# Precedence for VectorE's additions on read-outs of the projection, blocks 2 to 5, in a fused attention and SwiGLU kernel

## The chip, the cores and the metric

The kernel runs on one core of a Trainium2 chip. The metric is the device time of one execution in microseconds (us), as the median of several runs. The core's engines have a queue each: TensorE (PE; its weight loads are listed apart as PEld), VectorE (DVE), ScalarE (ACT), GpSimd (POOL) and SyncE (SP). Each queue is worked off in its own order, and semaphores hold an instruction until what it needs is done.

## The reference

```python
# q, k, v: (8, 8, 576, 64)  batch, heads, positions, head size; float32
scores = scale * q @ k.T                      # per batch and head
scores += -slope[h] * abs(i - j)              # ALiBi
attn = softmax(where(0 <= i - j < 128, scores, -1e9))
x = (attn @ v)  -> (4608, 512)                # tokens x (heads * head size)
g, val = x @ w_gate, x @ w_val                # 512 -> 1536
out = (g * sigmoid(g) * val) @ w_out          # 1536 -> 512
```

So it is a sliding-window attention of 128 positions, followed by a gated feed-forward block. The last product, 1536 to 512, is called the projection here.

## The kernel before

**Blocks.** The 4608 tokens are worked on as nine blocks of 512. The code counts them from 0 (`n`), this text from 1: blocks 2 to 5 are `n` = 1 to 4. For each block the attention makes `x`, which is transposed into `xT`. Then the gate (`pg`) and value (`pv`) products follow (L397, 128x512 tiles). ScalarE applies tanh (L415, `tt`). VectorE makes `uu = (tt + 1) * pg` (L416) and `hT = uu * pv` (L427).

**Projection with seven products.** From the second block on, the projection is done by a seven-product scheme in place of eight (the function `strassen`), in two passes `t` of 128 token columns each. It needs sums of parts of `hT`, which VectorE makes (L485 to L488, tiles `S2`, `S3`, `S4`, and in place in `hT`), and its seven products of six matmuls each (L532) read these sums. Pass by pass the products run so:

| product | into | read out by |
|---|---|---|
| first | `X` | ScalarE, to `p1s` |
| second | `p2`, a bank of its own | VectorE: `half_plus`, with `p1s` |
| third, on `S2` | `X`, added | ScalarE, to `u2s` |
| fourth | `Y` | ScalarE, to `p5s` |
| fifth, on `S3` | `X`, added | VectorE: `half_plus`, with `p5s` |
| sixth, on `S4` | `Y`, added | VectorE: `half_plus`, with `u2s` |
| seventh | `X`, added | ScalarE |

`X` and `Y` are the two halves of one PSUM bank:

```python
po = ps_f.tile([P, 2, HC], FP32, name="po", tag="po", bufs=1)
X, Y = po[:, 0, :], po[:, 1, :]
```

`p2` of blocks 2 to 5 comes from the pool `ps_a`, which has four banks. The same four banks hold the attention's scores (`ps` L278, `psc` L313) and its weighted values (`av` L345). VectorE frees an `av` bank with a reciprocal and a multiplication (L347, L348, tile `x`). VectorE also multiplies the exponentials with the mask (L290 `ex`, L321 `exc`). The products of block `n` - 1 are mixed into the gate and value products of block `n`, and attention for later blocks runs in between. Sums of weights (L597 to L600) are made on VectorE too, from the sixth block on in the program's text, into `kT`, `qT` and mask tiles that are no longer needed; they are read by products of blocks 7 to 9 (L623).

**Who sets the order.** A first part of the program, up to step 60 of the feed-forward steps, has a hand-written order on PE, VectorE and ScalarE. From there on, only PE's order is written by hand; the order on VectorE and ScalarE is chosen when the program is built, by a scheduler that takes, of the instructions that it holds to be ready, the one with the highest priority:

```python
fixed.enter_context(tc.manual_schedule(engines=ENGINES["pe"]))
```

Normally priority follows the order in which the program is written. `tc.high_priority()` lifts what is written under it above the rest. `half_plus` is L535 and L536.

Of the kernel before, what the change touches and what calls it, by code (L numbers as in the profile page):

```python
# [13 lines left out]
ALU = mybir.AluOpType  # L14
# [17 lines left out]
SEVEN_FROM = 6  # L32
# [19 lines left out]
def kernel(  # L52
# [10 lines left out]
    nc = tc.nc  # L63
# [377 lines left out]
    def store(n, j, osb, c0=0, c1=512, two=False):  # L441
        for i, (p0, p1, r0) in enumerate(rows_of(n, j)):
            (nc.scalar if two and i else nc.sync).dma_start(out[r0:r0 + p1 - p0, c0:c1],
                                                            osb[p0:p1, c0:c1])
# [59 lines left out]
    def strassen(n, t):  # L504

        h = hT[n]
        A11, A12 = h[:, 0:HM, 0:256], h[:, HM:NMB, 0:256]
        S1, A22 = h[:, 0:HM, 256:512], h[:, HM:NMB, 256:512]
        S2, S3, S4 = hsum[n]
        cols = slice(t * P, (t + 1) * P)  # L510
        end = n == NBLK - 1
        seeded = SEVEN_FROM <= n + 1 < NBLK
        factor = 1.0 if n >= SEVEN_FROM else 0.5
        if end:
            X, Y = (ps_a.tile([P, HC], FP32, name="po", tag="a", bufs=4) for _ in range(2))
            p2 = ps_f.tile([P, HC], FP32, name="p2", tag="gv")
        else:
            po = ps_f.tile([P, 2, HC], FP32, name="po", tag="po", bufs=1)
            X, Y = po[:, 0, :], po[:, 1, :]
            p2 = (ps_f.tile([P, HC], FP32, name="p2", tag="gv") if seeded  # L520
                  else ps_a.tile([P, HC], FP32, name="p2", tag="a"))
        top, low = (opool.tile([P, DM], FP32, name="osb", tag="osb") for _ in range(2))
        if end and t:
            spare = [opool.tile([P, DM], FP32, name="osb", tag="osb") for _ in range(2)]
            p1s, p5s, u2s = spare[0][:, 0:HC], spare[0][:, HC:DM], spare[1][:, 0:HC]
        else:
            p1s, p5s, u2s = (supool.tile([P, HC], FP32, name=i, tag=i, bufs=1)
                             for i in ("p1s", "p5s", "u2s"))

        def product(dst, a, b, start=False):  # L530
            for m in range(HM):
                nc.tensor.matmul(dst, a[:, m, cols], b[:, m, :], start=(start and m == 0),  # L532
                                 stop=(m == HM - 1), skip_group_check=True)

        def half_plus(dst, a, b):  # L535
            nc.vector.scalar_tensor_tensor(out=dst, in0=a, scalar=factor, in1=b,  # L536
                                           op0=ALU.mult, op1=ALU.add)

        product(X, A11, B11, True)
        if seeded:  # L540
            nc.scalar.copy(p2, X)
        else:
            nc.scalar.mul(p1s, X, factor)
        yield
        product(p2, A12, B21, not seeded)
        if seeded:
            nc.vector.tensor_scalar_mul(top[:, 0:HC], p2, factor)
        else:
            half_plus(top[:, 0:HC], p2, p1s)
        if end and t:  # L550
            store(n, t, top, 0, HC)
        yield
        product(X, S2, T2)
        nc.scalar.mul(u2s, X, factor)
        yield
        product(Y, S1, T1, end)
        if end and t:
            nc.vector.tensor_scalar_mul(p5s, Y, factor)
        else:
            nc.scalar.mul(p5s, Y, factor)  # L560
        yield
        product(X, S3, T3)
        half_plus(low[:, HC:DM], X, p5s)
        if end and t:
            store(n, t + 2, low, HC, DM, True)
        yield
        product(Y, S4, B22)
        half_plus(top[:, HC:DM], Y, u2s)
        store(n, t, top, HC if end and t else 0, DM, end)
        yield  # L570
        product(X, A22, T4)
        if end:
            nc.vector.tensor_scalar_mul(low[:, 0:HC], X, factor)
        else:
            nc.scalar.mul(low[:, 0:HC], X, factor)
        store(n, t + 2, low, 0, HC if end and t else DM, end)
        yield
# [427 lines left out]
```

## Time and profile before

| | before |
|---|---|
| median of 6 runs | 345.23 us (344.74 to 345.55) |
| profiled execution, time | 345.42 us |
| profiled execution, span in the trace | 343.6 us |
| PE busy | 329.9 us (96%) |
| VectorE busy | 277.4 us (81%) |
| ScalarE busy | 207.6 us (60%) |
| granted TensorE clock | 1.0 |

Times in the trace are counted from the start of the span. "Busy" is the time in which an engine works on something. A group of instructions is named by line, engine, operation and its tiles, out<-in. In a timeline, each row has the start, the time from the first start to the last end, the engine, line, operation, tiles and count, and in brackets the idle time of the engine before it with the instruction that ended it. The modelled ends of matmuls overlap the start of the next ones a little.

### The profile page before, as it was taken

What the parts mean: (1) busy time and instruction counts of PE and PEld (TensorE: products, weight loads), DVE (VectorE), ACT (ScalarE), POOL (GpSimd) and SP (SyncE); (2) the same over time, 40 slices, a digit from 0 to 9 for tenths busy, and PEclk for the clock granted to TensorE, in tenths of its full rate; (3) what the DMA queues carried; (4) which work ended last, traced back from release to release, by engine and by line L of the source; (5) the groups of instructions that cost most, each with busy time, mean ns of one, the idle gap of its engine ahead of it and who ended that gap; (6) DMA issues with size and microseconds to landing.
All of it is one profiled execution on the core that took longest, in us unless ns stands there. A gap on an engine that the chain in (4) does not pass through costs nothing.

```text
span 343.6 us, 7778 instructions
## 1 busy us (share of the span) xinstructions
PE 329.9 (96%) x2983; PEld 218.6 (64%) x2983; DVE 277.4 (81%) x652; ACT 207.6 (60%) x412; POOL 109.6 (32%) x136
## 2 busy tenths in 40 slices
PE   7999999999999999999999999999999999999995
PEld 3584445444456565556565655565788878888884
DVE  5477985999798669998899999999855875775683
ACT  3748676465766665656555547563467666776640
POOL 8977672648774274744017000000000000000000
PEclk9999999999999999999999999999999999999999
DMA  9999999999999999999999912021101101011014
GB/s 149 168 180 177 162 169 151 78 139 153 132 173 137 159 169 165 144 165 134 160 199 99 183 30 82 15 63 47 63 2 61 62 1 64 2 62 63 0 68 118
DMA packets 160037, 37.37 MB, mean 109 GB/s; under 512 B 147328, under 2 KB 155648, under 8 KB 160000
## 3 DMA queue, kind: packets, MB, share of 16 engines
q0 software_dynamic: 118336, 18.62, 85.5%
q1 hardware_dynamic: 40976, 17.64, 28.3%
q10 hardware_dynamic: 688, 0.62, 0.6%
q8 instruction: 23, 0.38, 0.5%
q14 instruction: 14, 0.11, 0.1%
HBM read 37.91 MB, written 9.44 MB: 138 GB/s over the span
## 4 chain that ended last, share of the span: by engine, by line
PE 68%; DVE 20%; ACT 6%; issue 3%; DMA 2%; SPq 0%; DVEq 0%; ACTq 0%
PE po L532 14%; PE pg L397 12%; PE pv L397 12%; PE gX L623 8%; PE gY L623 4%; PE av L345 4%; DVE uu L416 3%; DVE hT L427 3%; PE ps L278 3%; PE p L532 2%; DVE x L348 2%; PE gZ L623 2%; DVE ex L290 2%; ACT ex L284 2%; PE po L451 2%
## 5 line engine op out<-in xcount | busy, mean ns | idle before, releaser
L397 PE MATMUL pv<-xT,wv_sb 128*128 128x512 f16 (+2 forms) x320 | 76.5, 358 | 0.6 <-DVE uu L416 0.3
L397 PE MATMUL pg<-xT,wg_sb 128*128 128x512 f16 (+2 forms) x320 | 75.8, 358 | 0.3 <-DVE xT L373 0.2
L415 ACT ACTIVATE tt<-pg 128x512 f16<-128x512 f32 (+2 forms) x70 | 41.3, 590 | 50.5 <-PE pg L397 49.5
L284 ACT ACTIVATE ex<-ps 128x512 f16<-128x512 f32 x96 | 50.0, 606 | 12.0 <-PE ps L278 12.0
L416 DVE SCALAR_TENSOR_TENSOR uu<-tt,pg 128x512 f16<-128x512 f16 (+2 forms) x69 | 46.1, 668 | 10.4 <-ACT tt L415 10.2
L427 DVE TENSOR_TENSOR hT<-uu,pv 128x512 f16<-128x512 f16 (+2 forms) x70 | 46.8, 668 | 3.6 <-PE pv L397 1.6
L185 POOL DMA_DIRECT2D va<-in_v_dram x40 | 34.3, 861 | 34.4 <-PE av L345 26.9
L397 PEld LDWEIGHTS <-wg_sb 128*128 128x128 f16 x320 | 28.2, 98 | 24.4 <-issue 2.2
L397 PEld LDWEIGHTS <-wv_sb 128*128 128x128 f16 x320 | 28.3, 98 | 24.1 <-issue 3.0
L532 PEld LDWEIGHTS <-hT 128*128 128x128 f16 x384 | 36.8, 98 | 10.4 <-issue 1.1
L191 POOL DMA_DIRECT2D kn<-in_k_dram x39 | 33.2, 854 | 20.9 <-DMA kT<-kn 11.1
L191 POOL DMA_DIRECT2D qn<-in_q_dram x39 | 33.3, 860 | 19.7 <-DMA va<-in_v_dram 11.7
L532 PEld LDWEIGHTS <-S 128*128 128x128 f16 x288 | 27.7, 98 | 10.6 <-issue 2.5
L290 DVE TENSOR_TENSOR ex<-ex,m_reg 128x1024 f16<-128x1024 f16 x42 | 28.7, 689 | 3.2 <-ACT ex L284 3.1
L348 DVE TENSOR_TENSOR x<-av,rec 128x256 f16<-128x256 f32 x72 | 28.6, 420 | 0.4
L532 PE MATMUL po<-T,S 128*128 128x256 f16 x192 | 26.5, 273 | 0.5 <-DVE S L487 0.5
L532 PE MATMUL po<-T,hT 128*128 128x256 f16 x192 | 26.1, 273 | 0.0
L317 ACT ACTIVATE exc<-psc 128x512 f16<-128x512 f32 x40 | 21.3, 608 | 4.1 <-PE psc L313 4.1
L675 DVE TENSOR_TENSOR hT<-s,v 128x512 f16<-128x512 f16 x18 | 7.6, 425 | 18.5 <-ACT s L674 18.5
L345 PEld LDWEIGHTS <-ex 128*128 128x128 f16 x384 | 17.4, 97 | 4.6 <-issue 1.3
L345 PE MATMUL av<-va,ex 128*128 128x65 f16 x384 | 19.3, 193 | 0.7 <-ACT ex L284 0.7
L278 PE MATMUL ps<-qT,kT 64*128 64x256 f16 x192 | 16.6, 272 | 0.4 <-DVE qT L223 0.2
(134 smaller groups left out, 536.9 us busy)
## 6 DMA issues: line engine op xcount, KB each, us to landing
out_dram<-osb SPq DMA_DIRECT2D x32, 256.0 KB, 2.6
va<-in_v_dram POOLq DMA_DIRECT2D x32, 128.0 KB, 8.8
qn<-in_q_dram POOLq DMA_DIRECT2D x31, 128.0 KB, 8.8
kn<-in_k_dram POOLq DMA_DIRECT2D x31, 128.0 KB, 9.1
wg_sb<-in_moe_w_gate_dram POOLq DMA_DIRECT2D x6, 256.0 KB, 7.8
wv_sb<-in_moe_w_val_dram POOLq DMA_DIRECT2D x6, 256.0 KB, 8.3
wo_sb<-in_moe_w_out_dram POOLq DMA_DIRECT2D x2, 768.0 KB, 9.7
kn<-in_k_dram POOLq DMA_DIRECT2D x8, 64.0 KB, 7.2
```

Source lines behind the costliest of these rows:

```text
L185: nc.gpsimd.dma_start(va[rank][p0:p1, :, 0:D], src)
L191: nc.gpsimd.dma_start(t_[p0:p1], src)
L284: nc.scalar.activation(e[:, o:o + 2, :], banks[q4][par], AF.Exp, scale=scale)
L290: nc.vector.tensor_mul(e[:, o, :], e[:, o, :], reg[:, o, :])
L345: nc.tensor.matmul(av[:, j, :], w, val, start=(n == 0), stop=(n == len(todo) - 1))
L348: nc.vector.tensor_mul(x[:, 4 * half:4 * half + 4, :], av[:, :, 0:D], rec.broadcast_to([P, 4, D]))
L397: nc.tensor.matmul(ps[:, c0:c1], w[:, kb, ms], xT[n][:, kb, c0:c1], start=(kb == 0 and c0 == 0), stop=(kb == NKB - 1 and c1 == 512), skip_ ...
L415: nc.scalar.activation(tt, pg[:, c0:c1], AF.Tanh, scale=0.5)
L416: nc.vector.scalar_tensor_tensor(out=uu, in0=tt, scalar=one if (n, m) == PIN else 1.0, in1=pg[:, c0:c1], op0=ALU.add, op1=ALU.mult)
L427: nc.vector.tensor_mul(hT[n][:, m, c0:c1], acted[(n, m)][1][:, c0:c1], pv[:, c0:c1])
L532: nc.tensor.matmul(dst, a[:, m, cols], b[:, m, :], start=(start and m == 0), stop=(m == HM - 1), skip_group_check=True)
L623: nc.tensor.matmul(dst[:, i, :], w[:, kb, c0 + i * P:c0 + (i + 1) * P], a[:, kb, :], start=(start and i == 0 and kb == 0), stop=(i == 1 an ...
```

## The change

```diff
         def half_plus(dst, a, b):
-            nc.vector.scalar_tensor_tensor(out=dst, in0=a, scalar=factor, in1=b,
-                                           op0=ALU.mult, op1=ALU.add)
+            with tc.high_priority() if n + 1 < SEVEN_FROM else ExitStack():
+                nc.vector.scalar_tensor_tensor(out=dst, in0=a, scalar=factor, in1=b,
+                                               op0=ALU.mult, op1=ALU.add)
```

`SEVEN_FROM` is 6, so the 24 additions of `n` = 1 to 4 are lifted: four blocks, two passes, three additions each. The instructions of the program stay the same. In the built program the queues of PE, ScalarE, GpSimd and SyncE stand in the same order as before. On VectorE, the same 652 working instructions are there, and 93 of them stand at another place of the queue, between about 110 and 240 us of the trace before.

## The prediction

> **What bounds the kernel now.** I read the page first, then who waits for the changed line, then the stages, then both engines' timelines at each place where TensorE (PE) waits for VectorE.
>
> ```profile
> PE 329.9 (96%) x2983; PEld 218.6 (64%) x2983; DVE 277.4 (81%) x652; ACT 207.6 (60%) x412; POOL 109.6 (32%) x136
> PE 68%; DVE 20%; ACT 6%; issue 3%; DMA 2%; SPq 0%; DVEq 0%; ACTq 0%
> ```
>
> PE is busy for 96% of the span and carries 68% of the chain that ended last. VectorE carries 20% of it: there PE stood and waited for VectorE. PE's queue does not change, so the change can gain or lose only at such waits. The view of line 536 (the additions) ends with those who waited for it:
>
> ```profile
> who waited for it (us, times):
>   PE po L532: 1.5, 2
>   PE psc L313: 0.2, 1
> ```
>
> So three visible waits, 1.7 us together: about the most that this change can bring. The stages show how full VectorE is there (columns: window, length, then busy time and count of PE, PEld, DVE, ACT, POOL):
>
> ```profile
> 98.00:190.00 92.00, 89.81 (x841) 54.89 (x840) 81.72 (x190) 57.09 (x116) 42.05 (x51) 1.00 1.94 155
> 190.00:246.00 56.00, 55.33 (x480) 33.27 (x478) 54.39 (x135) 28.90 (x57) 0.00 (x0) 1.00 0.35 67
> ```
>
> PE idles for 2.2 us and 0.7 us in them; VectorE is busy for 54.39 of 56 us in the second. So an addition that goes first pushes back something that PE may need next. The waits, on PE:
>
> ```profile
> 167.55 0.39 PE L371 MATMUL px<-idm,x 128*128 128x128 f16 x4
> 168.56 0.82 PE L532 MATMUL po<-wo_sb,S 128*128 128x256 f16 x6 [0.62 <-DVE osb L536]
> ...
> 182.21 0.61 PE L278 MATMUL ps<-qT,kT 64*128 64x256 f16 x8
> ...
> 189.35 0.81 PE L532 MATMUL po<-wo_sb,S 128*128 128x256 f16 x6 [0.84 <-DVE osb L536]
> ...
> 218.65 0.39 PE L532 MATMUL po<-T,S 128*128 128x256 f16 x2 [0.52 <-DVE S L487]
> 218.98 0.45 PE L313 MATMUL psc<-qT,kT 64*128 64x128 f16 x9
> 219.58 0.38 PE L313 MATMUL psc<-qT,kT 64*128 64x128 f16 x7 [0.15 <-DVE osb L536]
> ```
>
> and VectorE's queue ahead of them:
>
> ```profile
> 141.73 0.42 DVE L487 TENSOR_TENSOR S<-hT 128x512 f16<-128x512 f16 x1
> 142.07 0.69 DVE L321 TENSOR_TENSOR exc<-exc,m_reg 128x1024 f16<-128x1024 f16 x1
> 142.67 0.42 DVE L536 SCALAR_TENSOR_TENSOR osb<-p,p1s 128x256 f32<-128x256 f32 x1
> ...
> 167.49 0.68 DVE L427 TENSOR_TENSOR hT<-uu,pv 128x512 f16<-128x512 f16 x1
> 168.08 0.42 DVE L536 SCALAR_TENSOR_TENSOR osb<-po,p5s 128x256 f32<-128x256 f32 x1
> ...
> 188.28 0.68 DVE L416 SCALAR_TENSOR_TENSOR uu<-tt,pg 128x512 f16<-128x512 f16 x1
> 188.88 0.42 DVE L536 SCALAR_TENSOR_TENSOR osb<-po,p5s 128x256 f32<-128x256 f32 x1
> ```
>
> The additions of the last two rows read `X` (with `p5s`). They stand behind an `uu` or `hT` step, while PE's next product waits to write `Y` in the same bank.
>
> **Slots.** Consecutive VectorE instructions start 0.085 us before the one ahead ends: 142.67 to 143.00 is a slot of 0.34 for an addition of 0.42, 168.08 less 167.49 is 0.59 for an `hT` of 0.68. PE's held instruction starts about 0.05 after VectorE's end (168.08 + 0.42 = 168.50, start 168.56). With these rows I follow the new order of VectorE's queue against the old and keep one number: PE's offset against before.
>
> **The change part by part.** It adds and removes no instruction; each of the 24 additions keeps its 0.42 us. Six places matter.
>
> A, 110.95 us: an addition passes a reciprocal (slot 0.09), and PE's wait of 0.03 ends. Offset -0.03.
>
> B, 141.73: the addition on `p2` is now put ahead of the sum `S2` (L487) and `exc`. `S2` comes 0.34 later, less the 0.02 of A. PE's weight loads of `S` are just in time now (six take 0.75 us at 141.65, and 0.53 at 168.56), so PE stands: offset +0.32. The next load that waits for an `x` step (at 144.03, idle 0.21 before it in PEld's timeline) finds it done as early as before, since all three moved steps stand ahead of it in both orders; that wait of 0.20 vanishes. Offset +0.12.
>
> C, 168.56: the addition passes `hT` (0.59), and VectorE is 0.12 late from B, because its last idle ahead (0.56 at 165.40) ends by ScalarE's `exc`, which follows PE. So it starts 0.47 earlier. PE's wait, start to start, is 168.56 less 167.55 less 0.28 (four such transposes at 110.64, next at 110.95, less A's 0.03) = 0.73. Of it 0.73 - 0.12 - 0.47 = 0.14 stays. Offset -0.47, a step of -0.59.
>
> D, 182.21: PE would come 0.47 early to the scores tile whose bank `x` frees at 181.80 + 0.42 = 182.22. VectorE shows no idle worth naming between 166 and 194, and this `x` has the same steps ahead of it in both orders (an `ex` half moves 2 us back, but still stands before it), so `x` cannot come earlier. The fifth weight load stands at about 182.34, only 0.06 after the release. So 0.41 is given back: offset -0.06.
>
> E, 189.35: the addition passes `uu` (0.60), and a weight sum (L597, 0.34) that stood ahead at 185.26 goes behind it. It starts near 187.96 and ends at 188.38, before PE needs it: the first load of `S` is at 188.44, its matmul 0.11 later (the spacing of these matmuls), so the product starts at 188.55 less D's 0.06 = 188.49 instead of 189.35. Offset -0.87, a step of -0.81.
>
> Is E kept? Behind it VectorE idles in the old order by 0.13, 0.45, 0.11, 0.31, 0.05 and 0.11 us at 194.62, 195.76, 196.90, 200.30, 201.71 and 205.21 (each start less the end before it), 1.16 in sum, and three of these end by ScalarE's `tt` or `exc`, which follow PE. That is room for 0.87.
>
> F, 218.65: the addition on `p2` passes eight steps, among them one `x` and `S2`. `S2` comes 0.87 - 0.33 = 0.54 earlier only, and PE waits longer for it: offset -0.54. In return the wait of `psc` for this addition ends. Matmuls of L313 follow each other by some 0.027 (sixteen in 0.62 at 105.70); the tenth stands at 219.58 instead of 218.98 + 9 x 0.027 = 219.22, so 0.36 is won. Offset -0.90.
>
> Behind 220 us no PE wait hangs on a moved step: the moved weight sums and sums of `xT` are read from 246 us on, and the masked `ex` half of D is written by 181.9 and read by PE's weighted values at 184.28 at the earliest. Stores of the output by SyncE follow the additions and wait for no one on the path. Sum: **-0.9 us**. The profiled execution took 345.42 (span 343.6 and 1.8 around it), and 0.19 over the median; I take the step from the median: 345.23 - 0.9 = **344.3**.
>
> Bounds: the smallest C + D is 0 (all given back), and E lies between 0 and 0.90 (the 0.84 of idle and the 0.06 of overlap). B + F lie between -0.4 (the S2 delays hidden) and +0.65 (no return of either). I take the worked values, since each rests on rows at its own place.
>
> [...] The row says that VectorE is busy for 54.39 of 56 us from 190 on and idles 1.16 us in 189 to 205. [...] I go by the idle row. In B and F the delay is a slot of 0.34 by the rows. [...]
>
> **The rivals.** (1) *Given back.* VectorE is full from 166 to 194 and nearly so to 240, and E's gain returns as PE's wait for `S2` at 218.65. For it: that wait exists, 0.52 us. Against it: the idle of 1.16. The time: -0.9 + 0.81 = -0.1, so 345.1. (2) *S2 pushed back, slower.* Additions go ahead of the sums that the next product reads, at B (+0.35, 0.20 of it returned) and F (+0.33, unreturned if `psc` is really held by something else). It decides if the waits of C and E were held by a second release close behind the addition, say ScalarE's copy of the same bank. Then the sum is -0.03 + 0.15 + 0.33 = +0.45: 345.7, and 345.9 if B's 0.20 does not return either. Against it: both rows name the addition, and PE starts 0.05 after its end. (3) *It does nothing.* The scheduler's order could already be best; but the queues differ at the named places. 345.2.
>
> **How the numbers follow.** The forecast has 0.76, rival 1 has 0.16, rival 2 has 0.05, rival 3 has 0.03. What a measurement of this kernel can tell from no change is about 0.2%, 0.69 us. The forecast's own range is 343.9 to 344.7; the six runs spread over 0.8, so a median may bring a fifteenth of its chance, 0.05, to within 0.2%. So faster 0.76 - 0.05 = 0.71; within 0.2% 0.05 + 0.16 + 0.03 = 0.24; slower 0.05. The range runs from 343.8 (the S2 delays hidden) up to the middle of rival 1, 345.1: it leaves out half of that rival, the other two and the forecast's edges, under 0.2 together.
>
> **What would show it.** Right: PE's idle before the products near 168 and 188.5 falls to at most 0.2 us and to none; `S2` waits of PE near 142 and 218 grow by 0.3; a new wait of L278's load for `x` near 182; the additions' row of waiters falls from 1.7 to about 0.2; PE's last instruction 0.9 us earlier. Wrong: E's place still held, by a ScalarE copy or a sum, or PE's offset against before returns to near 0 at 218.

## The result, and the profile after

| | before | after |
|---|---|---|
| median | 345.32 us (48 runs) | 344.17 us (23 runs) |
| ratio, 95% interval | | 0.9969 (0.9959 to 0.9978) |
| span of the profiled execution | 343.6 us | 342.7 us |

The change saves 1.07 us by the ratio (0.76 to 1.42); the two medians differ by 1.15. The forecast was 0.9.

In the page after, PE is as busy as before in microseconds, in a shorter span, and the chain that ended last holds less of VectorE (17% for 20%):

```profile
PE 329.7 (96%) x2983; PEld 218.6 (64%) x2983; DVE 276.8 (81%) x652; ACT 207.6 (61%) x412; POOL 109.6 (32%) x136
PE 66%; DVE 17%; DMA 10%; issue 3%; ACT 2%; POOL 1%; ACTq 0%; DVEq 0%; POOLq 0%
```

The view of the additions' line, now 537, names no one any more who waited for it; before it named PE with 1.5 and 0.2 us. The stages (same columns as before) show PE busy 1.25 us longer from 98 to 190, with VectorE as before:

```profile
who waited for it (us, times):
busy tenths in 40 slices 0000000000000000000000000000000000000011
```

```profile
98.00:190.00 92.00, 91.06 (x846) 55.23 (x845) 81.67 (x190) 57.42 (x117) 41.37 (x50) 1.00 1.77 155
190.00:246.00 56.00, 55.15 (x484) 33.76 (x483) 54.82 (x137) 29.09 (x59) 0.00 (x0) 1.00 0.27 67
```

Now the six places, first VectorE's queue. At B the addition stands ahead of `S2`, at C ahead of `hT`, at E ahead of `uu`, with the weight sum (now L598) behind it:

```profile
141.53 0.42 DVE L537 SCALAR_TENSOR_TENSOR osb<-p,p1s 128x256 f32<-128x256 f32 x1
141.87 0.42 DVE L487 TENSOR_TENSOR S<-hT 128x512 f16<-128x512 f16 x1
...
167.44 0.41 DVE L537 SCALAR_TENSOR_TENSOR osb<-po,p5s 128x256 f32<-128x256 f32 x1
167.77 0.68 DVE L427 TENSOR_TENSOR hT<-uu,pv 128x512 f16<-128x512 f16 x1
...
187.79 0.42 DVE L537 SCALAR_TENSOR_TENSOR osb<-po,p5s 128x256 f32<-128x256 f32 x1
188.13 0.68 DVE L416 SCALAR_TENSOR_TENSOR uu<-tt,pg 128x512 f16<-128x512 f16 x1
188.72 0.42 DVE L598 TENSOR_TENSOR qT<-wv_sb,wg_sb 128x512 f16<-128x512 f16 x1
```

PE's weight loads, where the two new waits are (B and D):

```profile
142.34 0.11 PEld L532 LDWEIGHTS <-S 128*128 128x128 f16 x2 [0.36 <-DVE S L487]
...
181.59 0.22 PEld L278 LDWEIGHTS <-kT 64*128 64x128 f16 x5 [0.42 <-issue]
182.12 0.11 PEld L278 LDWEIGHTS <-kT 64*128 64x128 f16 x3 [0.31 <-DVE x L348]
```

and PE at C, E and F:

```profile
167.49 0.39 PE L371 MATMUL px<-idm,x 128*128 128x128 f16 x4
167.91 0.82 PE L532 MATMUL po<-wo_sb,S 128*128 128x256 f16 x6
...
188.27 0.81 PE L532 MATMUL po<-wo_sb,S 128*128 128x256 f16 x6
...
217.90 0.39 PE L532 MATMUL po<-T,S 128*128 128x256 f16 x2 [0.85 <-DVE S L487]
218.22 0.62 PE L313 MATMUL psc<-qT,kT 64*128 64x128 f16 x16
```

The idle of 0.62 and 0.84 us at C and E is gone. PE's wait for `S2` at F has grown from 0.52 to 0.85, and the sixteen `psc` matmuls run through.

**One caution in reading.** Single profiled executions differ in their first 60 us, where no instruction has moved: the `pv` product at 109.78 before starts at 109.65 after, 0.13 earlier, and in the experiments' traces 0.2 to 0.7 earlier. So I compare the starts of the same matmul (PE's queue is the same in all kernels) and take off the offset that it has at that `pv`. Second traces of two of the kernels (the full change and the additions after the fifth product, both run again below) repeat their rows of the table within 0.03 us. The offset behind each place, in us:

| behind place | A | B | C | D | E | F | last matmul |
|---|---|---|---|---|---|---|---|
| forecast | -0.03 | +0.12 | -0.47 | -0.06 | -0.87 | -0.90 | -0.90 |
| after | -0.07 | +0.07 | -0.52 | -0.19 | -0.96 | -0.99 | -0.99 |
| additions after the fifth product | -0.07 | -0.08 | -0.68 | -0.65 | -1.13 | -1.14 | -1.16 |
| additions on `p2` | 0.00 | +0.14 | +0.14 | +0.30 | +0.13 | +0.09 | +0.16 |
| place C alone | 0.00 | -0.01 | -0.61 | -0.58 | -0.47 | -0.47 | -0.48 |
| place E alone | 0.00 | -0.01 | -0.01 | -0.01 | -0.62 | -0.62 | -0.64 |

The lower rows belong to the experiments that follow.

### The profile page after: what moved, and what is told of

It reads as the page before. It is cut to its first block, busy times and chain, and to the rows that moved or that the text cites. A ratio compares the mean times of both kernels' runs of the same rounds, so it can differ in the third digit from the quotient of the medians.

```text
span 342.7 us, 7780 instructions
## 1 busy us (share of the span) xinstructions
PE 329.7 (96%) x2983; PEld 218.6 (64%) x2983; DVE 276.8 (81%) x652; ACT 207.6 (61%) x412; POOL 109.6 (32%) x136
## 4 chain that ended last, share of the span: by engine, by line
PE 66%; DVE 17%; DMA 10%; issue 3%; ACT 2%; POOL 1%; ACTq 0%; DVEq 0%; POOLq 0%
PE po L532 15%; PE pv L397 12%; PE pg L397 12%; PE gX L624 8%; DMA qn<-in_q_dram 6%; PE gY L624 4%; PE av L345 3%; DMA va<-in_v_dram 3%; PE ps L278 2%; PE p L532 2%; DVE hT L427 2%; DVE uu L416 2%; PE gZ L624 2%; DVE ex L290 2%; DVE x L348 2%
## 5 line engine op out<-in xcount | busy, mean ns | idle before, releaser
L290 DVE TENSOR_TENSOR ex<-ex,m_reg 128x1024 f16<-128x1024 f16 x42 | 28.9, 688 | 3.4 <-ACT ex L284 3.3
L278 PE MATMUL ps<-qT,kT 64*128 64x256 f16 x192 | 16.7, 272 | 0.4 <-DVE qT L223 0.2
```

The source lines that it names most:

```text
L290: nc.vector.tensor_mul(e[:, o, :], e[:, o, :], reg[:, o, :])
```

## Experiments: which additions bring it

The theory says that each lifted addition moves PE's waits by its slot on VectorE, at the places named. The rival of count says that any addition lifted frees its PSUM bank sooner and brings its share.

**Only after the fifth product.**

```diff
-        def half_plus(dst, a, b):
-            with tc.high_priority() if n + 1 < SEVEN_FROM else ExitStack():
+        def half_plus(dst, a, b, lift):
+            with tc.high_priority() if lift else ExitStack():
...
+            half_plus(top[:, 0:HC], p2, p1s, False)
...
+        half_plus(low[:, HC:DM], X, p5s, 1 <= n <= 4)
...
+        half_plus(top[:, HC:DM], Y, u2s, False)
```

> Only the additions after the fifth product (with p5s) are lifted in blocks 2 to 5; those on p2 (with p1s) and after the sixth product (with u2s) stay where they were. Theory (places): the gain sits at C (near 168) and E (near 189), and both are additions after the fifth product; the losses at B (near 142), D (near 182) and F (near 218) come from additions on p2. So C gives -0.6, some 0.15 of it is returned before E, E gives -0.6, nothing is lost at B and F: -1.0 to -1.1 us against before, as good as the full change or 0.15 better. Rival (count): each lifted addition frees a PSUM bank sooner and brings about the same; a third of the additions, a third of the full change's gain: -0.3 us.

Measured: 343.75 us against 345.09, ratio 0.9962 (0.9949 to 0.9974). In its PE timeline E keeps a wait of 0.24: PE comes there earlier than in the full change (offset behind D -0.65 for -0.19), and the addition on VectorE does not start earlier by as much (0.16). The waits of F stand as before, only earlier:

```profile
187.51 0.82 PE L532 MATMUL po<-wo_sb,S 128*128 128x256 f16 x6 [0.24 <-DVE osb L537]
...
216.80 0.39 PE L532 MATMUL po<-T,S 128*128 128x256 f16 x2 [0.52 <-DVE S L487]
217.13 0.45 PE L313 MATMUL psc<-qT,kT 64*128 64x128 f16 x9
217.73 0.38 PE L313 MATMUL psc<-qT,kT 64*128 64x128 f16 x7 [0.15 <-DVE osb L537]
```

At D almost nothing is returned, 0.03 us where the expectation had some 0.15 before E and the full change returned 0.33. VectorE's queue shows why: one masked exponential (L290) stands right ahead of the `x` that PE waits for in the full change, and behind it here. So this `x` starts 0.79 us earlier than before (landmark taken off), and 0.03 earlier in the full change. First the full change, then this kernel:

```profile
181.07 0.66 DVE L290 TENSOR_TENSOR ex<-ex,m_reg 128x1024 f16<-128x1024 f16 x1
181.65 0.42 DVE L348 TENSOR_TENSOR x<-av,rec 128x256 f16<-128x256 f32 x1
...
180.30 0.41 DVE L348 TENSOR_TENSOR x<-av,rec 128x256 f16<-128x256 f32 x1
180.63 0.68 DVE L290 TENSOR_TENSOR ex<-ex,m_reg 128x1024 f16<-128x1024 f16 x1
```

A third of the additions brings at least the whole gain. The rival of count falls.

**Only on p2.** The same edit, with the lift on the other line:

```diff
+            half_plus(top[:, 0:HC], p2, p1s, 1 <= n <= 4)
...
+        half_plus(low[:, HC:DM], X, p5s, False)
```

> Only the additions on p2 (with p1s) are lifted in blocks 2 to 5. Theory (places): S2 comes a slot of 0.34 later at B and at F, and a step ahead of the x that PE waits for at D comes first; no wait of C and E ends sooner. B +0.35 less 0.20 returned, D up to +0.3 which E's wait takes back, F +0.33 less 0.36 returned, and up to 0.1 more behind it: slower by 0.1 to 0.3 us. PE waits for S2 near 142 and 218 by 0.3 longer than before. Rival (count): -0.3 us, because the bank of p2 goes back to the attention's pool sooner.

Measured: 345.17 us against 345.09, ratio 1.0002 (0.9993 to 1.0011), so the times don't tell the loss from zero. Its offset in the table, +0.16 at the last matmul, is a loss of the expected kind and lies within that interval. The trace has the three longer waits, for `S2` at B and F and for `x` at D (weight loads twice, then PE):

```profile
141.94 0.11 PEld L532 LDWEIGHTS <-S 128*128 128x128 f16 x2 [0.35 <-DVE S L487]
...
182.15 0.11 PEld L278 LDWEIGHTS <-kT 64*128 64x128 f16 x3 [0.17 <-DVE x L348]
...
218.52 0.39 PE L532 MATMUL po<-T,S 128*128 128x256 f16 x2 [0.84 <-DVE S L487]
```

**One addition each.**

```diff
+        half_plus(low[:, HC:DM], X, p5s, (n, t) == (2, 1))
```

> One addition alone is lifted: block 3 (n = 2), second pass, after the fifth product; it passes one hT step of 0.59. Theory (places): PE's product near 168 starts 0.59 earlier; later waits for VectorE, which is full from 166 to 194, return some 0.15 of it: -0.45 us. Rival (count): one of 24 additions, -0.04 us. Rival (given back): VectorE is full behind C, so all of it comes back: 0.

Measured: 344.59 against 345.09, ratio 0.9985 (0.9976 to 0.9993), which is -0.5 us (-0.2 to -0.8).

```diff
+        half_plus(low[:, HC:DM], X, p5s, (n, t) == (3, 0))
```

> One addition alone is lifted: block 4 (n = 3), first pass, after the fifth product; it passes one uu step of 0.60. Theory (places): PE's product near 189 starts 0.60 earlier and keeps it, since VectorE has 1.16 us of idle behind it up to 205: -0.6 us. Rival (count): -0.04 us. Rival (given back): 0, with PE's wait for S2 near 218 longer by 0.6.

Measured: 344.48 against 345.09, ratio 0.9978 (0.997 to 0.9987), which is -0.8 us (-0.4 to -1.0); the medians differ by 0.6. In both runs the rivals' times lie outside the interval. The offsets are -0.48 and -0.64. With A's -0.07 they add up to -1.19, and the kernel with all eight additions after the fifth product has -1.16. So two additions of the 24 carry the gain. The eight after the sixth product (with `u2s`) have no run of their own; -1.16 and the +0.16 of those on `p2` add up to -1.00, and the full change has -0.99, so next to nothing is left for them if the parts add up.

**Is the narrower lift better?** The kernel with the fifth-product additions alone was run again beside the full change, on one chip.

> The kernel with the additions after the fifth product alone lifted, once more, on one chip with the full change. Theory (places): 0.1 to 0.2 us under the full change, because S2 is not pushed back at B and F and the x of D keeps its place. Rival (count): 0.6 us slower than the full change.

> The full change once more, for a comparison on one chip: -0.9 to -1.1 us against before by either theory.

Measured: 344.06 and 344.04 us against 345.11; ratios 0.9965 (0.9952 to 0.9979) and 0.9969 (0.9957 to 0.998). In the traces it is 0.12 us ahead (last matmul -1.14 and -1.02); the times can't tell the two apart. It beats the kernel before, and is not shown to beat the change.

## Experiments: does VectorE need room behind the gain?

Rival 1 of the prediction said that a full VectorE gives the gain back. The added work writes two weight sums of two column groups three times each:

```diff
+        def again(out, x, y):
+            for _ in range(3 if u in (0, 1) else 1):
+                nc.vector.tensor_sub(out, x, y)
...
+        return [lambda: again(t1, V1[:, :, cols], G1[:, :, cols]),
+                lambda: again(t3, V2[:, :, cols], V1[:, :, cols]),
```

> The kernel before with more work on VectorE: two of the weight sums (L597 and L598) of two column groups are written three times each with the same values, eight instructions of 0.34 us a slot, 2.7 us in all, which the scheduler puts mostly between 184 and 240 us. Nothing is lifted. Theory (room): VectorE's idle time behind 189 takes most of them, and what is over shows as longer waits of PE: +0.5 us (0.2 to 1.2) against before. Rival (VectorE's time counts in full there): +2.7 us.

> The same eight added instructions, with all 24 additions lifted as in the changed kernel. Theory (room): the gain of E is kept only because VectorE has idle time behind it; filled up, PE's wait for S2 near 218 and the waits behind it take E's gain back. What stays of the gain against the filled kernel without lifting is 0.2 to 0.4 us in place of 0.9 to 1.1: +0.2 us against before. Rival (no room needed): the full gain against the filled kernel, so 0.9 to 1.1 us under it: -0.5 us against before.

> The same eight added instructions, with the additions after the fifth product alone lifted. Theory (room): as with all lifted, 0.3 us under the filled kernel without lifting and no more: +0.2 us against before. Rival (no room needed): 1.0 us under it: -0.5 us against before.

| with the eight instructions added | us, before 345.16 | ratio (interval) | offset behind E | at 205 | behind F | last matmul |
|---|---|---|---|---|---|---|
| nothing lifted | 345.59 | 1.0013 (1.0004 to 1.0021) | 0.00 | 0.00 | +0.01 | +0.44 |
| all 24 lifted | 345.38 | 1.0006 (0.9997 to 1.0014) | -0.96 | -0.92 | -0.24 | +0.11 |
| after the fifth product | 345.21 | 1.0002 (0.9993 to 1.001) | -1.11 | -1.06 | -0.36 | +0.07 |

With nothing lifted, the 2.7 us of added work cost 0.44, near the expected 0.5. With lifting, the gain is there behind E, as large as without the added work, and two thirds of it are lost by the last matmul: of 0.99 and 1.16 us, 0.33 and 0.37 stay (0.44 less 0.11 and 0.07). The times alone give 0.2 and 0.4 with wide intervals, but they leave out the rival's -0.5 against before in both kernels. PE of the kernel with all lifted shows where the gain goes, into waits for VectorE near 205 and 218, which take 0.43 and 0.29 us of it:

```profile
205.51 0.81 PE L532 MATMUL po<-wo_sb,S 128*128 128x256 f16 x6 [0.32 <-DVE osb L537]
...
218.22 0.39 PE L532 MATMUL po<-T,S 128*128 128x256 f16 x2 [1.19 <-DVE S L487]
...
241.51 0.81 PE L532 MATMUL po<-wo_sb,S 128*128 128x256 f16 x6 [0.18 <-DVE osb L537]
```

The third wait, near 241, is a cost of the added work itself: with nothing lifted it stands too, and is longer.

```profile
241.80 0.82 PE L532 MATMUL po<-wo_sb,S 128*128 128x256 f16 x6 [0.27 <-DVE osb L537]
```

The idle time of VectorE between 189 and 205 is what is used up. In this window it is busy for 14.95 us before, 15.59 after the change, and 15.90 with the change and the added work (third busy time of each row, in this order):

```profile
189.00:205.00 16.00, 15.65 (x146) 9.73 (x146) 14.95 (x36) 8.83 (x18) 0.00 (x0) 1.00 0.95 108
189.00:205.00 16.00, 16.00 (x147) 9.49 (x147) 15.59 (x38) 8.42 (x18) 0.00 (x0) 1.00 0.58 97
189.00:205.00 16.00, 16.00 (x151) 9.57 (x149) 15.90 (x40) 8.31 (x18) 0.00 (x0) 1.00 0.54 86
```

So the mechanism of rival 1 is real, and what kept most of it from happening is VectorE's idle time behind E.

## Experiment: lift what PE waits for at F

```diff
-        return four_sums(a11, a12, a21, a22, s2, s3, s4)
+        def lifted(f):
+            with tc.high_priority() if n == 4 else ExitStack():
+                f()
+        return [lambda f=f: lifted(f) for f in four_sums(a11, a12, a21, a22, s2, s3, s4)]
```

> No addition is lifted; in their place the sums of hT for block 5's projection (L485 to L488, n = 4), which PE waits for at F, are. Theory (slots): what is lifted goes ahead of steps that PE needs sooner. An addition near 206 stands behind a row of sums then, and PE's product waits for it by about 2 us; half of it comes back as PE no longer waits for S2 near 218: slower by 1 us (0.5 to 1.5). Rival (precedence for what PE visibly waits for always helps): PE's wait of 0.52 for S2 goes: -0.4 us.

Measured: 346.81 us against 345.16, ratio 1.0043 (1.0025 to 1.006). Seven sums stand ahead of the addition with `p5s` (in the view's rows: three, two and two), and PE waits 1.96 us for it. The first two fences are VectorE and PE; the third is the view by windows:

```profile
205.59 1.09 DVE L485 TENSOR_TENSOR S<-hT 128x512 f16<-128x512 f16 x3
206.59 0.76 DVE L486 TENSOR_TENSOR hT<-hT 128x512 f16<-128x512 f16 x2
207.26 0.76 DVE L487 TENSOR_TENSOR S<-hT 128x512 f16<-128x512 f16 x2
207.93 0.42 DVE L540 SCALAR_TENSOR_TENSOR osb<-po,p5s 128x256 f32<-128x256 f32 x1
```

```profile
204.88 1.03 PE L397 MATMUL pg<-xT,wg_sb 128*128 128x512 f16 x4
205.83 0.61 PE L278 MATMUL ps<-qT,kT 64*128 64x256 f16 x8
208.40 0.98 PE L535 MATMUL po<-wo_sb,S 128*128 128x256 f16 x6 [1.96 <-DVE osb L540]
209.18 1.91 PE L397 MATMUL pv<-xT,wv_sb 128*128 128x512 f16 x4
```

```profile
205.00:209.00 4.00, 2.04 (x19) 1.12 (x17) 4.00 (x11) 2.56 (x5) 0.00 (x0) 0.99 0.16 33
209.00:213.00 4.00, 4.00 (x22) 2.01 (x20) 3.13 (x9) 0.11 (x1) 0.00 (x0) 0.58 0.17 66
```

The wait of 2 us came as expected. Its price was higher than expected: four matmuls of `pv` take 1.91 us where four of `pg` took 1.03 ahead of it, and the granted clock is 0.58 from 209 to 213. In this trace the offset is +2.02 at the held product (208.40 for 206.60 before, 0.22 taken off for the landmark) and grows to +3.65 at the next product, on `hT` (212.69 for 209.26), ahead of which the clock was lowered; 1.02 comes back by the product at 242.86 (240.45 before), as the expectation had it (half of 2), and +2.63 is left at the last matmul. Without the 1.63 that it grew by, that would be +1.00. The eight timed runs fall in two groups, four from 345.91 to 346.15 (0.8 to 1.0 over before) and four from 347.47 to 348.18 (2.3 to 3.0 over). The first group lies at the expected +1.0, with mean granted clocks of 0.998 to 1.0. In the second, three runs have 0.994, the traced one among them, which fits a lowered stretch; the fourth, 347.93 us, has 0.999, and its time stays unexplained. The rival, that lifting what PE visibly waits for always helps, falls in either.

## Why the prediction was right

- *Which places count.* All six behaved in the forecast's direction, and no seventh appeared: the steps were -0.07, +0.14, -0.59, +0.33, -0.77 and -0.03 us against -0.03, +0.15, -0.59, +0.41, -0.81 and -0.03. They sum to -0.99 in place of -0.90.
- *D was the term that was mis-sized.* I put the release at the fifth weight load of L278, at 182.34. The row after shows five loads that go ahead and the sixth that stands. Its matmul comes at 182.45 in the trace before, 0.11 behind the time that I used, and `x` ended 0.03 earlier than before, so the slack was near 0.2 us and not 0.06 (the table keeps 0.19), and 0.33 was returned for 0.41. That `x` could not come earlier holds only for the order that the full change got: with the additions after the fifth product alone it came 0.79 earlier. A's wait was worth 0.07 for 0.03.
- *C and E* were held by the addition alone, as the rows said; single additions there bring 0.6 at the place. In the full change E gives 0.77 for 0.62. There the weight sum went behind the addition (188.72), where in the kernel with place E alone it still stands ahead and PE keeps a wait of 0.25. The addition starts 0.96 earlier than before in the full change and 0.61 earlier in that kernel, and the difference, 0.35, is about the slot of that sum; it was not tested by itself.
- *Rival 1* did not happen, and the filled kernels show its condition. VectorE's busy time from 190 to 246, 54.39 of 56 us before, did not hold the gain back, but with the eight added instructions and nothing lifted it was 55.43, and with them two thirds of the gain were lost. So 1.0 of the last 1.6 us of idle made the difference.
- *Rival 2* has a true part: precedence for the additions on `p2` delays `S2` by a slot at B and F. F costs nothing only because the wait of `psc` ends in return. The slot at F is 0.33 by the rows (`x`, `S2` start 1.08 and 0.75 earlier than before), where the forecast had 0.34.

## What to carry to other kernels

When one engine's queue stays fixed and another's is reordered, list the waits of the first for the second, and price each move as a slot at that wait: what goes ahead, what PE needs that goes behind, and where the pushed-back engine has idle time to catch up. Here a gain upstream was kept where the reordered engine had idle time before the next wait for it, and mostly lost where that time was filled. Lift the two or three instructions that a wait names and read what each one passes: here the other lifts brought nothing that could be measured, and in the traces they cost 0.1 to 0.2 us.

## What the runs showed of the hardware that was not expected

A single idle stretch of PE of 1.96 us (206.44 to 208.40 in the trace with block 5's sums lifted) was followed by a lowered granted clock: 0.99 from 205 to 209, 0.58 from 209 to 213, and 1.00 again from 213 to 217. The four `pv` matmuls behind the held product take 1.71 us up to the start of the next group (209.18 to 210.89), for 0.86 before (207.27 to 208.13): half the pace. With a clock of 0.5 for the lowered stretch, the two windows give it a length of about 3.4 us, an estimate from these numbers: 0.01 and 0.42 of 4 us each, doubled.

The waits of 0.84 us before and of 1.19 us with the added work and all 24 lifted were not followed by a lowered clock: in both traces it is 1.00 from 98 to 190 and from 190 to 246. From 205 to 209, with the wait of 1.96 us, PE was busy for 2.04 of 4 us. That the idle time caused the lowered clock is not shown: it rests on one trace, and one of the untraced runs of the change (346.12 us, the slowest) also has a lowered mean clock, 0.992.
